# A local-attention and star-ReLU feed-forward kernel: hand-fixed issue order, DMA transposes, and the position bias added by TensorE

## The chip, the cores and the metric

The kernel runs on one core of a Trainium2 chip. The metric is device time in microseconds (us) for one execution. The span that a profile prints (first to last instruction) is about 2 us shorter than that time. An execution is called *slow* when it is over 1.5% above the fastest of the same kernel, otherwise *fast*. The engines are named as in the profile: PE is TensorE, PEld its weight loads (which overlap PE: 155.4 and 242.9 us busy in a span of 263.5 before), DVE is VectorE, ACT is ScalarE, POOL is GpSimd, SP is SyncE. An engine with a q (SPq, POOLq) is the engine issuing DMAs.

## The reference, cut to what matters

Four batches, 8 heads, 768 positions, 64 elements a head. A query sees the first 8 positions (global) and the 96 positions up to itself (local), with a linear penalty on distance that depends on the head. The attention output, put together over the heads to 3072 rows of 512, goes through a two-layer feed-forward network.

```python
scores = q @ k.T / 8
keep   = (pos_k < 8) | ((rel >= 0) & (rel < 96))        # rel = pos_q - pos_k
dist   = where(global and not local, 96, |rel|)
scores = where(keep, scores - slope[h] * dist, -1e9)     # slope[h] = 2 ** -(h + 1)
a      = softmax(scores)
x      = (a @ v) put together over heads                 # 3072 x 512
h      = x @ w_in                                        # 512 -> 2048
out    = (s * relu(h) ** 2 + b) @ w_out                  # 2048 -> 512
```

## The kernel before

It works on 12 *granules*: 256 query positions of one batch, all 8 heads, so 3 granules a batch. A granule is done in four *steps*, one for each pair of heads. In a step PE transposes q and k of the pair that comes two steps later, makes the scores of the next pair, multiplies probabilities and values for this one, and does a quarter of the hidden layer (P1) of the granule before and a quarter of the output layer (P2) of the one before that. The instructions are written in this order, and a scheduler may move them.

```python
    for s in range(NSTEP):                       # four steps a granule
        jm, qd = s // HP, s % HP
        if qd == 0:
            load_granule(*pend_loads.pop(0))     # GpSimd queue, fp32 to bf16
            make_voff(jm + 1)
        run_S(s + 1)                             # scores, exp, times template
        moe_p1(jm - 1, 2 * qd)
        mms, norm = stage_A(s); mms(); norm()    # probabilities x values
        moe_p1(jm - 1, 2 * qd + 1)
        run_T(s + 2)                             # 4 PE transposes, DVE evacuates
        moe_p2(jm - 2, qd // 2, qd % 2)
    # [conditions at the ends cut]

    # stage_A: lhsT, loaded into PE beforehand as its weights, is called stationary; rhs moves
    # here the values are stationary (64 columns: half the array), 128 queries move
    nc.tensor.matmul(av[hi*D:(hi+1)*D, i*P:(i+1)*P], lhsT=vv,
                     rhs=pts[hi][:, c*P:(c+1)*P], ...)          # 8 a step
    # ... and again with ones, for the row sums
    nc.tensor.matmul(av[hi*D:(hi+1)*D, GT+i*P:GT+(i+1)*P], lhsT=ones_bf[:, 0:D],
                     rhs=pts[hi][:, c*P:(c+1)*P], ...)          # 8 a step
    # norm: xT = av * exp(-ln(sum)), already transposed for P1
    nc.scalar.activation(lg[:], av[:, GT:2*GT], ACT.Ln)
    nc.scalar.activation(rc[:], lg[:], ACT.Exp, scale=-1.0)
    nc.vector.tensor_tensor(xT[j][:, hp, :], av[:, 0:GT], rc[:], ALU.mult)

    # start: the loads are one queue, in this order
    load_granule(0, 0)
    for i in range(4): load_w_in(i, 4)
    # [8 templates exp(-slope * dist) on ACT]
    load_granule(0, 1)
    for i in range(4): load_w_out(i, 4)
    load_granule(0, 2)
```

The softmax here doesn't subtract the row's maximum and nothing guards it: scores larger than these inputs give would overflow.

Of the kernel before, what the change touches and what calls it, by code (L numbers as in the profile page):

```python
# [8 lines left out]
F32 = mybir.dt.float32  # L9
# [4 lines left out]
NEG_BIG = -30000.0  # L14


@with_exitstack
def kernel(
# [23 lines left out]
    NGR = S // GT  # L42
    HP = H // 2
# [3 lines left out]
    NU = NJ * HP  # L47
# [8 lines left out]
    ldp = ctx.enter_context(tc.tile_pool(name="ldp", bufs=2))  # L56
    qkp = ctx.enter_context(tc.tile_pool(name="qkp", bufs=2))
    work = ctx.enter_context(tc.tile_pool(name="work", bufs=3))
    ppool = ctx.enter_context(tc.tile_pool(name="ppool", bufs=8))
    gpool = ctx.enter_context(tc.tile_pool(name="gpool", bufs=2))  # L60
    xpool = ctx.enter_context(tc.tile_pool(name="xpool", bufs=3))
    ps_sc = ctx.enter_context(tc.tile_pool(name="ps_sc", bufs=3, space=bass.MemoryType.PSUM))
    ps_av = ctx.enter_context(tc.tile_pool(name="ps_av", bufs=2, space=bass.MemoryType.PSUM))
    ps_h = ctx.enter_context(tc.tile_pool(name="ps_h", bufs=3, space=bass.MemoryType.PSUM))

    nc.scalar.preload_act_table_set("natural_log_exp_and_others")


    nat = {}
    for b in range(B):  # L70
        for nm in ("q", "k", "v"):
            nat[nm, b] = None

    def load(nm, src, b, g, h0, nh):
        key = (nm, b)
        if nat[key] is None:
            nat[key] = ldp.tile([P, S // P, H, D], BF16, name=f"{nm}nat", tag=f"{nm}nat")
        t = nat[key]
        for sb in range(g * GB, (g + 1) * GB):
            nc.gpsimd.dma_start(  # L80
                t[:, sb, h0 : h0 + nh, :],
                src[b, h0 : h0 + nh, sb * P : (sb + 1) * P, :].rearrange("h p d -> p h d"),
            )
# [4 lines left out]
    w_out_view = moe_w_out.rearrange("(fc p) c -> p fc c", p=P)  # L88

# [6 lines left out]
    def load_w_out(i, n):  # L96
        w = FC // n
        nc.gpsimd.dma_start(
            w_out_bf[:, i * w : (i + 1) * w, :], w_out_view[:, i * w : (i + 1) * w, :]
        )  # L100

    def load_granule(b, g, parts=1):
        n = H // parts
        for h0 in range(0, H, n):
            load("k", k, b, g, h0, n)
            load("q", q, b, g, h0, n)
            load("v", v, b, g, h0, n)

    s_bc = const.tile([P, 1], F32, name="s_bc")
    nc.sync.dma_start(s_bc[:], moe_s.to_broadcast((P, 1)))  # L110
    b_bc = const.tile([P, 1], F32, name="b_bc")
    nc.sync.dma_start(b_bc[:], moe_b.to_broadcast((P, 1)))

    ident_bf = const.tile([P, P], BF16, name="ident_bf")
    make_identity(nc, ident_bf[:])
    ones_bf = const.tile([P, P], BF16, name="ones_bf")
    nc.vector.memset(ones_bf[:], 1.0)


    base = const.tile([P, 5, P], F32, name="base")  # L120
# [8 lines left out]

# [8 lines left out]
    )  # L138
    nc.gpsimd.affine_select(
        out=rel[:],  # L140
# [7 lines left out]
    load_granule(0, 0)  # L148
    for i in range(4):
        load_w_in(i, 4)  # L150

    for i in (0, 1, 4):
        nc.vector.tensor_copy(base[:, i, :], rel[:, 0:P])
    for i in (2, 3):
        nc.vector.tensor_copy(base[:, i, :], rel[:, P : 2 * P])
    nc.vector.tensor_scalar_max(base[0:NG, 0, :], base[0:NG, 0, :], -float(NL))
    nc.vector.memset(base[0:NG, 2:4, :], -float(NL))

    tmpl = []
    for h in range(H):  # L160
        t = const.tile([P, 5 * P], BF16, name=f"tmpl{h}", tag=f"tmpl{h}")
        slope = float(2.0 ** (-8.0 * (h + 1) / H))
        nc.scalar.activation(
            t[:], base[:].rearrange("p a c -> p (a c)"), ACT.Exp, scale=slope
        )
        tmpl.append(t)

    load_granule(0, 1)
    for i in range(4):
        load_w_out(i, 4)  # L170
    load_granule(0, 2)


    st = {}
    qk = {}
    xT = {}
    gT = {}

    def unit(u):
        j, hp = divmod(u, HP)  # L180
        b, g = divmod(j, NGR)
        return j, hp, b, g

    voff_tiles = {}

    def make_voff(j):
        b, g = divmod(j, NGR)
        vn = nat["v", b]
        if g == 0:
            return  # L190
        vo = work.tile([P, GB, H, D], BF16, name="voff", tag="voff", bufs=2)
        nc.vector.tensor_copy(vo[:], vn[:, g * GB - 1 : (g + 1) * GB - 1, :, :])
        for i in range(GB):
            nc.vector.tensor_copy(vo[0:NG, i, :, :], vn[0:NG, 0, :, :])
        voff_tiles[j] = vo

    def stage_T(u):
        j, hp, b, g = unit(u)
        ps = ps_h.tile([P, 4 * P], BF16, name="ps_t", tag="psh")
        qn, kn = nat["q", b], nat["k", b]  # L200
        ops = []
        for i in range(GB):
            ops.append(
                lambda i=i: nc.tensor.transpose(  # L204
                    ps[:, (GB + i) * P : (GB + i + 1) * P],
                    kn[:, g * GB + i, 2 * hp : 2 * hp + 2, :],
                    ident_bf[:],
                )
            )
        for i in range(GB):  # L210
            ops.append(
                lambda i=i: nc.tensor.transpose(  # L212
                    ps[:, i * P : (i + 1) * P],
                    qn[:, g * GB + i, 2 * hp : 2 * hp + 2, :],
                    ident_bf[:],
                )
            )
        t = qkp.tile([P, 4 * P], BF16, name="qk", tag=f"qk{hp}_{g}")
        qk[b, g, hp] = t

        def evac():
            nc.vector.tensor_copy(t[:], ps[:])  # L222
            if g > 0:
                ko = work.tile([P, GB, P], BF16, name="koff", tag="koff", bufs=4)
                prev = qk[b, g - 1, hp]
                nc.vector.tensor_copy(ko[:, 0, NG:], prev[:, 3 * P + NG : 4 * P])  # L226
                nc.vector.tensor_copy(ko[:, 1, NG:], t[:, 2 * P + NG : 3 * P])
                first = qk[b, 0, hp]
                nc.vector.tensor_copy(
                    ko[:, :, 0:NG],  # L230
                    first[:, 2 * P : 2 * P + NG].unsqueeze(1).to_broadcast((P, GB, NG)),
                )
                st[u] = {"ko": ko}
            else:
                st[u] = {}

        return ops, evac



    def stage_S(u):
        j, hp, b, g = unit(u)
        t = qk[b, g, hp]
        first = g == 0
        ncol = 3 * P if first else 4 * P
        pss = [ps_sc.tile([P, 4 * P], F32, name="ps_s", tag="sc") for _ in range(2)]
        pts = [ppool.tile([P, 4 * P], BF16, name="pt", tag="pt") for _ in range(2)]
        st[u]["pt"] = pts

        def mms():  # L250
            if first:
                plan = [
                    (t, 2 * P, 0, 0),
                    (t, 3 * P, P, 1),
                    (t, 2 * P, P, 2),
                ]
            else:
                ko = st[u]["ko"][:].rearrange("p a c -> p (a c)")
                plan = [
                    (t, 2 * P, 0, 0),  # L260
                    (t, 3 * P, P, 3),
                    (ko, 0, 0, 1),
                    (ko, P, P, 2),
                ]
            for kt, kc0, qc0, oc in plan:
                for hi in range(2):
                    r0 = hi * D
                    nc.tensor.matmul(  # L268
                        pss[hi][:, oc * P : (oc + 1) * P],
                        lhsT=kt[r0 : r0 + D, kc0 : kc0 + P],  # L270
                        rhs=t[r0 : r0 + D, qc0 : qc0 + P],
                        start=True,
                        stop=True,
                    )

        def post(hi):
            h = 2 * hp + hi
            nc.scalar.activation(  # L278
                pts[hi][:, 0:ncol], pss[hi][:, 0:ncol], ACT.Exp, scale=QSCALE
            )  # L280
            m = tmpl[h][:, 0 : 3 * P] if first else tmpl[h][:, P : 5 * P]
            nc.vector.tensor_tensor(  # L282
                pts[hi][:, 0:ncol], pts[hi][:, 0:ncol], m, ALU.mult
            )

        return mms, [lambda: post(0), lambda: post(1)]

    def stage_A(u):
        j, hp, b, g = unit(u)
        first = g == 0  # L290
        pts = st[u]["pt"]
        vn = nat["v", b]
        vo = None if first else voff_tiles[j]
        av = ps_av.tile([P, 4 * P], F32, name="ps_av", tag="av")
        if j not in xT:
            xT[j] = xpool.tile([P, KC, GT], BF16, name="xT", tag="xT")
# [118 lines left out]
    def run_T(u):  # L415
        ops, evac = stage_T(u)
        for op in ops:
            op()
# [71 lines left out]
```

## Time and profile before

| | us |
|---|---|
| time, first listing (median of 3; lowest to highest) | 263.11 (263.06 to 266.51) |
| span of the profiled run | 263.5 |
| first P1 matmul starts | 23.55 |
| length of a step, 80 to 230 us | 4.80 (19.2 a granule) |
| last P2 matmul ends | about 259 |

These are lines of the page of the kernel before: busy time by engine, the busy tenths of PE and of DMA in 40 slices of 6.6 us, the granted clock, and the chain of work that ended last.

```profile
PE 242.9 (92%) x2376; PEld 155.4 (59%) x2416; DVE 152.7 (58%) x441; ACT 144.7 (55%) x297; POOL 71.1 (27%) x89
...
PE   0573999999999999999999999999999999999993
...
PEclk9999999999999999999999999999999999999998
DMA  6999999999991100159990110110011011011112
...
PE 89%; DMA 5%; POOL 3%; issue 1%; DVE 0%; ACT 0%; POOLq 0%
```

PE is busy 92% of the span and makes up 89% of the chain. No other engine is above 59%. So PE's own work is the time, apart from the start: PE is at 0, 5, 7 and 3 tenths in the first four slices. The chain in order of time names the reason (start, length, what):

```profile
10.59 12.72 DMA knat<-in_k_dram
```

The k of granule 1 stands in the queue behind all of w_in, and the chain holds 12.7 us from the issue of its load to its landing at 23.3. In this time PE still has some work; it stands idle for the last 4.6 us (its starts are at 18.49 and 23.36). The 9s of the PEclk row are misleading early on. The records of the granted clock begin at 39.6 us; before that P1 and transposes start twice as far apart as later (128-column matmuls 107 ns instead of 55 to 56), so PE ran at half its later rate.

The window 150 to 200 us gives busy time for PE, PEld, DVE, ACT, POOL (instruction counts in brackets), then granted clock, DMA share and GB/s:

```profile
150.00:200.00 50.00, 49.52 (x520) 32.32 (x529) 32.51 (x95) 30.94 (x65) 0.00 (x0) 1.00 0.08 28
```

PE is busy 49.5 of 50 us. This is one step there, PE only (start, length, line, operation, output<-inputs, shape, count):

```profile
153.62 0.28 PE L268 MATMUL ps_s<-qk 64*128 64x128 bf16 x4
...
153.94 1.05 PE L355 MATMUL ps_2471<-xT,w_in_bf 128*128 128x256 bf16 x8
154.92 0.25 PE L316 MATMUL ps_av<-pt,vnat 128*64 128x128 bf16 x2
...
155.17 0.39 PE L329 MATMUL ps_av<-pt,ones_bf 128*64 128x128 bf16 x8
155.49 1.05 PE L355 MATMUL ps_2504<-xT,w_in_bf 128*128 128x256 bf16 x8
156.38 0.28 PE L204 MATMUL ps_t<-ident_bf,knat 128*128 128x128 bf16 x2
156.49 0.28 PE L212 MATMUL ps_t<-ident_bf,qnat 128*128 128x128 bf16 x2
156.60 1.89 PE L389 MATMUL ps_2526<-w_out_bf,gT 128*128 128x512 bf16 x7
158.42 0.28 PE L268 MATMUL ps_s<-qk 64*128 64x128 bf16 x4
```

Read the starts, not the lengths (the ends are modelled and overlap). The 16 matmuls for values and row sums (L316, L329) take from 154.92 to 155.49, 0.57 us. The transposes (L204, L212) take 0.22 us. Where half-array matmuls (64 in one dimension of the tile) meet full ones, the next start comes 0.15 to 0.20 us later instead of 0.06 to 0.11: at 153.94 after the scores, for example.

### The profile page before, as it was taken

How to read it: one execution, taken by the hardware profiler on the slowest of the kernel's cores; microseconds unless marked ns; L12 is line 12 of the kernel's file. 1: busy time of each engine (PE TensorE's matmuls, PEld its weight loads, DVE VectorE, ACT ScalarE, POOL GpSimd, SP SyncE). 2: the span in 40 equal slices, each digit the busy share in tenths (PEclk: the TensorE clock that was granted, in tenths of full speed). 3: DMA queues.
4: the chain of work that ended last, by engine and by line, in shares of the span. 5: the costliest groups of instructions: out<-in, count | busy, mean ns of one | idle time of the engine just before them, and what ended most of it. 6: DMA issues, size and time to landing. Idle time of an engine off the chain costs nothing.

```text
span 263.5 us, 5861 instructions
## 1 busy us (share of the span) xinstructions
PE 242.9 (92%) x2376; PEld 155.4 (59%) x2416; DVE 152.7 (58%) x441; ACT 144.7 (55%) x297; POOL 71.1 (27%) x89
## 2 busy tenths in 40 slices
PE   0573999999999999999999999999999999999993
PEld 0352565756666566666666666656666566666641
DVE  2440746777856676577575676567657567543331
ACT  4770454857557476575665756646556466463310
POOL 9945649859910000069700000000000000000000
PEclk9999999999999999999999999999999999999998
DMA  6999999999991100159990110110011011011112
GB/s 43 145 206 167 206 182 155 151 110 141 160 141 40 44 29 14 40 36 164 179 106 0 44 40 2 40 42 21 21 40 44 0 42 44 0 42 40 40 42 80
DMA packets 82875, 20.31 MB, mean 77 GB/s; under 512 B 75680, under 2 KB 79776, under 8 KB 82848
## 3 DMA queue, kind: packets, MB, share of 16 engines
q0 software_dynamic: 79104, 13.64, 69.3%
q1 hardware_dynamic: 3744, 6.29, 6.5%
q8 instruction: 19, 0.31, 0.5%
q14 instruction: 8, 0.07, 0.1%
HBM read 27.26 MB, written 6.29 MB: 127 GB/s over the span
## 4 chain that ended last, share of the span: by engine, by line
PE 89%; DMA 5%; POOL 3%; issue 1%; DVE 0%; ACT 0%; POOLq 0%
PE ps_s L268 6%; PE ps_av L316 6%; DMA knat<-in_k_dram 5%; PE ps_av L329 4%; PE ps_t L204 2%; PE ps_t L212 2%; PE ps_3986 L389 1%; PE ps_4006 L389 1%; PE ps_3944 L389 1%; PE ps_3006 L389 1%; PE ps_1081 L389 1%; PE ps_b L371 1%; PE ps_2048 L389 1%; PE ps_3880 L389 1%; PE ps_3793 L389 1%; PE ps_3642 L389 1%
## 5 line engine op out<-in xcount | busy, mean ns | idle before, releaser
L278 ACT ACTIVATE pt<-ps_s 128x512 bf16<-128x512 f32 (+1 forms) x96 | 49.0, 559 | 70.2 <-PE ps_s L268 70.1
L355 PEld LDWEIGHTS <-w_in_bf 128*128 128x128 bf16 x768 | 69.4, 100 | 18.4 <-issue 1.4
L389 PEld LDWEIGHTS <-gT 128*128 128x128 bf16 x384 | 36.0, 98 | 35.0
L364 DVE TENSOR_TENSOR gT<-gT 128x512 bf16<-128x512 bf16 x96 | 40.7, 424 | 22.8 <-ACT gT L363 21.0
L80 POOL DMA_DIRECT2D knat<-in_k_dram x24 | 21.9, 930 | 47.4 <-PE ps_t L212 44.1
L342 DVE TENSOR_TENSOR xT<-ps_av,rc 128x256 bf16<-128x256 f32 x48 | 20.3, 422 | 13.7 <-ACT rc L341 13.7
L204 PE MATMUL ps_t<-ident_bf,knat 128*128 128x128 bf16 x96 | 14.5, 233 | 11.1 <-DMA knat<-in_k_dram 11.1
L222 DVE COPY qk<-ps_t 128x512 bf16<-128x512 bf16 x48 | 19.7, 415 | 7.9 <-PE ps_t L212 7.9
L80 POOL DMA_DIRECT2D vnat<-in_v_dram x24 | 21.2, 908 | 6.3 <-DMA w_in_bf<-in_moe_w_in_dram 2.6
L80 POOL DMA_DIRECT2D qnat<-in_q_dram x24 | 21.5, 913 | 0.4 <-issue 0.3
L341 ACT ACTIVATE rc<-lg 128x256 f32<-128x256 f32 x48 | 20.0, 416 | 1.4
L316 PE MATMUL ps_av<-pt,vnat 128*64 128x128 bf16 x224 | 19.6, 241 | 1.2 <-DVE pt L282 0.7
L268 PEld LDWEIGHTS <-qk 64*128 64x128 bf16 x224 | 7.6, 97 | 21.1 <-issue 16.2
L339 ACT ACTIVATE lg<-ps_av 128x256 f32<-128x256 f32 x48 | 18.4, 383 | 2.5 <-PE ps_av L329 2.5
L329 PE MATMUL ps_av<-pt,ones_bf 128*64 128x128 bf16 x352 | 19.5, 230 | 0.0
L268 PE MATMUL ps_s<-qk 64*128 64x128 bf16 x224 | 17.8, 233 | 0.3 <-DVE qk L222 0.3
L204 PEld LDWEIGHTS <-knat 128*128 128x128 bf16 x96 | 9.5, 102 | 13.5 <-DMA knat<-in_k_dram 11.6
L316 PEld LDWEIGHTS <-vnat 128*64 128x64 bf16 x224 | 10.7, 114 | 11.1 <-issue 10.6
L212 PE MATMUL ps_t<-ident_bf,qnat 128*128 128x128 bf16 x96 | 14.3, 234 | 1.3 <-DMA qnat<-in_q_dram 1.3
L329 PEld LDWEIGHTS <-ones_bf 128*64 128x64 bf16 x352 | 14.1, 118 | 0.0
L226 DVE COPY koff<-qk 128x120 bf16<-128x120 bf16 x32 | 7.3, 234 | 8.9 <-PE ps_s L268 8.9
L282 DVE TENSOR_TENSOR pt<-pt,tmpl_136 128x512 bf16<-128x512 bf16 (+1 forms) x12 | 4.8, 403 | 11.5 <-ACT pt L278 11.5
(284 smaller groups left out, 389.7 us busy)
## 6 DMA issues: line engine op xcount, KB each, us to landing
out_dram<-o_sb SPq DMA_DIRECT2D x24, 256.0 KB, 2.0
knat<-in_k_dram POOLq DMA_DIRECT2D x24, 128.0 KB, 6.5
qnat<-in_q_dram POOLq DMA_DIRECT2D x24, 128.0 KB, 6.5
vnat<-in_v_dram POOLq DMA_DIRECT2D x24, 128.0 KB, 6.7
w_in_bf<-in_moe_w_in_dram POOLq DMA_DIRECT2D x4, 512.0 KB, 9.9
w_out_bf<-in_moe_w_out_dram POOLq DMA_DIRECT2D x4, 512.0 KB, 10.7
s_bc<-in_moe_s_dram SPq DMA_DIRECT2D x1, 0.5 KB, 2.8
b_bc<-in_moe_b_dram SPq DMA_DIRECT2D x1, 0.5 KB, 2.9
```

Source lines behind the costliest of these rows:

```text
L80: nc.gpsimd.dma_start(t[:, sb, h0 : h0 + nh, :], src[b, h0 : h0 + nh, sb * P : (sb + 1) * P, :].rearrange("h p d -> p h d"),)
L204: lambda i=i: nc.tensor.transpose(ps[:, (GB + i) * P : (GB + i + 1) * P], kn[:, g * GB + i, 2 * hp : 2 * hp + 2, :], ident_bf[:],)
L222: nc.vector.tensor_copy(t[:], ps[:])
L268: nc.tensor.matmul(pss[hi][:, oc * P : (oc + 1) * P], lhsT=kt[r0 : r0 + D, kc0 : kc0 + P], rhs=t[r0 : r0 + D, qc0 : qc0 + P], start=True, ...
L278: nc.scalar.activation(pts[hi][:, 0:ncol], pss[hi][:, 0:ncol], ACT.Exp, scale=QSCALE)
L316: nc.tensor.matmul(av[hi * D : (hi + 1) * D, i * P : (i + 1) * P], lhsT=vv, rhs=pts[hi][:, c * P : (c + 1) * P], start=not off, stop=bool( ...
L329: nc.tensor.matmul(av[hi * D : (hi + 1) * D, GT + i * P : GT + (i + 1) * P], lhsT=ones_bf[:, 0:D], rhs=pts[hi][:, c * P : (c + 1) * P], st ...
L341: nc.scalar.activation(rc[:], lg[:], ACT.Exp, scale=-1.0)
L342: nc.vector.tensor_tensor(xT[j][:, hp, :], av[:, 0:GT], rc[:], ALU.mult)
L355: nc.tensor.matmul(ps[:, i, :], lhsT=w_in_bf[:, kc, fc * P : (fc + 1) * P], rhs=xT[j][:, kc, :], start=(kc == 0), stop=(kc == KC - 1),)
L364: nc.vector.tensor_tensor(gs, gs, gs, ALU.mult)
L389: nc.tensor.matmul(po[:], lhsT=gT[j][:, fc, tb * P : (tb + 1) * P], rhs=w_out_bf[:, fc, :], start=(fc == 0), stop=(fc == FC - 1),)
```

## The change

The intent is to shorten the period and the start at once:

1. **Issue order by hand.** The order of the whole program is written out, and the scheduler is switched off. One *period* a granule replaces four steps.
2. **q and k transposes move to DMA**, two granules ahead, on SP's queue, from granule 3 on.
3. **Probabilities become stationary.** The output is queries by 65: 64 values and a 65th column of ones, which yields the row sum. Full-array matmuls, half as many, and a 4-column reciprocal on DVE in place of Ln and Exp on ACT. The result now has queries on partitions, so it must be transposed for P1: two more DMA transposes a granule (`xT`).
4. **Start.** Granule 1 loads before w_in, w_in comes in eighths; q and k of granules 0 to 2 are loaded in 512-byte runs (two positions at once); for granules 0 and 1 PE adds the position bias into PSUM with a scaled identity, so no template is multiplied; dummy matmuls before the first work are meant to end the half rate early.
5. **Output bias.** The sum over w_out is added up on DVE and finished with 2 matmuls instead of 16; POOL adds it to the first four output tiles, whose P2 finishes before it is known.

```diff
+    ctx.enter_context(tc.manual_schedule())
@@ loads at the start
-    load_granule(0, 0)
-    for i in range(4):
-        load_w_in(i, 4)
+    load_pairs(0, "k")  ...  load_pairs(0, "q")  ...  load_v(0)
+    load_pairs(1, "k"); load_pairs(1, "q"); load_v(1)
+    for i in range(8):
+        load_w_in(i, 8)
+    load_pairs(2, "k"); load_pairs(2, "q"); load_v(2)
+    # [w_out in quarters, granule 3]
+    load_granule(4)
@@ position bias of granules 0 and 1
+            nc.tensor.matmul(ps[:, hi, 0:n], lhsT=diag[:, 2 * hp + hi, :], rhs=m, start=True, stop=False)
@@ transposes of q and k (k shown)
-        nc.tensor.transpose(ps[...], kn[:, g * GB + i, 2 * hp : 2 * hp + 2, :], ident_bf[:])
+            nc.sync.dma_start_transpose(
+                kT[b][:, :, sb * P : (sb + 1) * P],
+                nat["k", j][:, i, :, :].rearrange("p h d -> p (h d)"))
@@ attention
-        nc.tensor.matmul(av[...], lhsT=vv,               rhs=pts[hi][:, c * P : (c + 1) * P], ...)
-        nc.tensor.matmul(av[...], lhsT=ones_bf[:, 0:D],  rhs=pts[hi][:, c * P : (c + 1) * P], ...)
+        nc.tensor.matmul(av[:, i, hi, :], lhsT=pt[:, hi, c * P : (c + 1) * P], rhs=vv, ...)   # 65 columns
-        nc.scalar.activation(lg[:], av[:, GT : 2 * GT], ACT.Ln)
-        nc.scalar.activation(rc[:], lg[:], ACT.Exp, scale=-1.0)
+        nc.vector.reciprocal(rc[:], av[:, :, :, D : D + 1])
+    def XT_dma(j):                                       # attention output, one granule
+        for i in range(GB):
+            nc.sync.dma_start_transpose(xT[j][:, :, i * P : (i + 1) * P], xn[j][:, i, :, :]...)
@@ the period
+    def period(j, items, at, late=None):
+        if j + 3 < NJ:
+            load_granule(j + 3)
+        SS(j, (0, 1)); run(items, at[0]); A(j, 0); run(items, at[1]); A(j, 1)
+        KO(j + 1); VO(j + 1)
+        SS(j, (2, 3)); run(items, at[2]); A(j, 2); run(items, at[3]); A(j, 3)
+        XT_dma(j)
+        XB(j + 2)                                        # q, k transposes by DMA
+        if late is not None: late()                      # output bias, granules 0, 1
+        run(items, 100)                                  # items: P1 of j-1, P2 of j-2 and j-1
```

(`...` and brackets mark cuts, and conditions at the ends are left out.)

## The prediction

It was written with the trace before and the diff at hand, before anything of the change was built.

> **What bounds it now.** TensorE. The page: PE busy 92% of 263.5 us, the chain 89% PE; DVE 58%, ACT 55%. From 80 to 230 us the windows have PE busy 98-99%; the timeline there repeats a step of 4.80 us, four steps a granule: 19.2 us, 12 granules. From matmul starts: 64 hidden-layer matmuls (256 columns) at 109 ns = 7.0 us; 32 output matmuls (512 columns) about 216 ns = 6.9; scores 16 pairs at 56 ns = 0.9; attention-value and ones-sums 32 pairs at 56 = 1.8; 16 transposes at 56 = 0.9. Sum 17.5. The other 1.7 us: entering or leaving half-array matmuls (scores, and values and sums) shows starts 0.15-0.20 us apart instead of 0.06-0.11. [...]four changes a step.
> The rest is the start: the chain has 12.7 us waiting for k of granule 1, behind all of w_in; the first hidden-layer matmul is at 23.5 us; starts are twice as far apart (107 ns instead of 56) until 39.6 us.
>
> **What changes.**
> - Steady PE: transposes go to DMA (-0.9 us a granule). Probabilities stationary: 32 full-array matmuls of 65 columns replace 64 half-array ones, the ones-sums going into a 65th column. The trace has a weight load plus 128-column matmul each 55 ns; for 65 columns I estimate 35-55 ns, so 1.1-1.8 us, against 1.8. Tiling changes fall from 16 to 4 (-1.2 us). Ideal 16.3-17.0 us a granule; with some stalls 17.1 (-2.1).
> - Ln and Exp normalisation (ACT 383+416 ns) becomes a small DVE reciprocal. DVE per granule, from durations: about 12 us; ACT about 9; neither binds a 17 us period.
> - Output bias sum: 16 matmuls of 512 (3.5 us) become 2.
> - Start: granule 1 loads before w_in; w_in in eighths lets the first hidden-layer pair begin after one eighth. Before, q/k/v of a granule moved in about 5 us, w_in in 10. So the first eighth lands about 12-13 us, the last about 21. 512-byte runs halve q/k packets early: 1-2 us. [...]PE bias removes early template multiplies, but ACT is busy: dense PE work from about 15-16 us.
> - New DMA: six transposes of 128 KB per granule on SP. No transpose is in this trace; stores of 256 KB land in 2.0 us. [...]k/q are two granules ahead. Only attention output (two in sequence) is tight: between the last attention matmuls and its first use lie about 6 us of PE work. I allow 0.5 us of stall per granule.
>
> **Sum.** 15.5 + hidden and output work 167 + attention of 10 granules 27 + granules 1-2 extras, transposes, bias 6 + start stalls 4 + transpose stalls 4 + tail 4.3 (as before) = 228 us. Range 219 to 241. Faster by over 2% 0.91; within 2% 0.05; slower 0.04.
>
> **What would show it.** First hidden-layer matmul near 15 us; twice-as-far starts ending well before 39 us; period of 16.5-17.5 us; no PE transposes after granule 2; fewer 0.15-0.20 us gaps; 65-column matmuls 35-55 ns apart; PE waits on attention-output transposes under 1 us each.
>
> **What would make it wrong.** Transposes landing in over 5 us, or SP issuing them slowly, stalls every granule; single-buffered score or output PSUM stalling a fixed order; weights arriving late, leaving PE holes up to 40 us.

The sum: 15.5 + 167 + 27 + 6 + 4 + 4 + 4.3 = 227.8, given as 228 us. Two of its figures are estimates: the 0.5 us of stall a granule, made with one landing time at hand (2.0 us for a store), and the 1 to 2 us for 512-byte runs (half the packets of q and k, in loads that took about 5 us a granule).

## The result, and the profile after

| | before | changed |
|---|---|---|
| time, us (median; lowest to highest) | 264.31 (263.06 to 266.51) | 236.58 (232.74 to 239.12) |
| ratio of fast runs | 1 | 0.886 (0.875 to 0.896) |
| first P1 matmul starts | 23.55 | 17.67 |
| period of a granule, steady part | 19.2 | 16.1 to 16.6 |
| PE waiting for `xT` | none | 8.8 |

A ratio is the mean time of one kernel's fast runs over the mean of the other's fast runs of the same rounds, with a 95% interval, so it isn't quite the ratio of the medians in the table. The changed kernel is 10 to 12.5% faster. Its own runs scatter more than those of any other kernel here: 237.22, 235.95, 239.12 and 232.74, with a mean granted clock of 0.971, 0.975, 0.961 and 0.992. The scatter is in the clock: span times (1 - clock), an estimate of the time lost to half rate, is 6.8, 5.9, 9.3 and 1.8 us, and without it the four spans are within 228.0 to 229.2 us. Two of the runs, the profiled one included, count as slow, so its share of half rate is higher than that of a fast run. What I read from this profile I therefore also looked for in fast profiles: one with different load runs at the start (`rows`, below) shows the same three waits.

The page of the changed kernel, the lines that answer to those of before (slices of 5.9 us):

```profile
PE 212.3 (90%) x1967; PEld 141.6 (60%) x1997; DVE 135.0 (57%) x311; ACT 115.1 (49%) x173; POOL 76.4 (32%) x95
...
PE   5899999985988899399999999999999999999993
...
PEclk9799999996799999979999999999999999999999
DMA  6999999999992899999589599423504413013102
...
PE 72%; DMA 10%; DVE 10%; ACT 3%; issue 3%; SPq 0%; DVEq 0%; POOLq 0%
```

PE's work fell from 242.9 to 212.3 us. PE is busy from the first slice, but there are now gaps in slices 10, 13 and 17. The clock is lower in slices 10, 11 and 18, right after, and in slice 2 (half rate from 6.9 to 10.3 us). Two entries of the chain have grown: DMA from 5 to 10%, DVE from 0 to 10%. In the steady part the window and the timeline of PE read:

```profile
150.00:200.00 50.00, 48.49 (x464) 33.93 (x471) 31.12 (x75) 25.73 (x37) 0.00 (x0) 1.00 0.33 82
```

```profile
160.25 0.19 PE L385 MATMUL ps_av<-vaug,pt 128*128 128x65 bf16 x1
160.28 0.20 PE L385 MATMUL ps_av<-vo,pt 128*128 128x65 bf16 x1
...
160.47 0.19 PE L385 MATMUL ps_av<-vo,pt 128*128 128x65 bf16 x1
160.50 1.91 PE L432 MATMUL ps<-xT,w_in_bf 128*128 128x256 bf16 x16
162.46 2.54 PE L473 MATMUL ps<-w_out_bf,gT 128*128 128x512 bf16 x11
```

The eight matmuls of a pair of heads take from 160.25 to 160.50, 0.25 us instead of 0.57, each with a fresh stationary tile and 29 to 35 ns apart. The long P2 group at 162.46 recurs at 178.58, 195.16 and 211.69 in the chain: a period of 16.1, 16.6 and 16.5 us.

What is left is in the list of waits of PE (total, times, longest):

```profile
PE ps L432 <- DMA xT<-xn: 8.8, 3, 4.0
PE ps L473 <- DVE o_sb L484: 3.2, 10, 0.5
```

All of the 8.8 us fall before 98 us: PE starts are 3.87 us apart at 51.8, 1.66 at 75.5 and 4.35 at 93.7. This is the last of the three, all engines (timeline, most lines cut):

```profile
88.46 1.81 POOL L103 DMA_DIRECT2D knat<-in_k_dram  x2
88.73 2.57 SPq L419 DMA_TRANSPOSE xT<-xn  x2
...
89.70 2.54 PE L473 MATMUL ps<-w_out_bf,gT 128*128 128x512 bf16 x11
90.19 1.83 POOL L103 DMA_DIRECT2D qnat<-in_q_dram  x2
...
91.92 1.85 POOL L111 DMA_DIRECT2D vaug<-in_v_dram  x2
...
93.08 1.02 PE L473 MATMUL ps<-w_out_bf,gT 128*128 128x512 bf16 x4 [0.29 <-DVE o_sb L484]
...
98.08 0.60 PE L432 MATMUL ps<-xT,w_in_bf 128*128 128x256 bf16 x4 [3.97 <-DMA xT<-xn]
```

SP issues the two `xT` transposes of granule 4 from 88.73 on, and at the same moment POOL issues the six loads of granule 7 (k, q, v). PE runs out of other work at about 94.1 and stands until 98.08. The DMA view says what these transposes need as a rule (issues, median us to landing):

```profile
xT<-xn SPq DMA_TRANSPOSE x20, 2.5
kT<-knat SPq DMA_TRANSPOSE x18, 3.1
qT<-qnat SPq DMA_TRANSPOSE x18, 3.5
```

The median of 2.5 us would have brought the second of them, issued at 89.98, home at 92.5, before PE needed it. It landed at 97.9. Each pair, with the packets of loads (GpSimd queue) that moved while it was under way, counted in the DMA records of the trace:

| `xT` of granule | issued at, us | landed after, us | load packets meanwhile |
|---|---|---|---|
| 2 | 46.01, 47.24 | 7.79, 8.41 | 5,622, 5,977 |
| 3 | 73.32, 74.56 | 2.42, 2.48 | 0, 16 |
| 4 | 88.73, 89.98 | 6.85, 7.96 | 4,972, 6,102 |
| 5 to 11 | | 2.4 to 3.1 | at most 268 |

The three waits are not all alike. The pair of granule 3 landed fast, beside no loads, and PE still waited 1.3 us for it:

```profile
73.32 2.51 SPq L419 DMA_TRANSPOSE xT<-xn  x2
...
77.18 1.03 PE L432 MATMUL ps<-xT,w_in_bf 128*128 128x256 bf16 x8 [1.29 <-DMA xT<-xn]
```

From the issue of its second transpose (74.56) to the end of PE's other work lie 1.3 us; in granule 4 it was 4.1 us. So this wait is one of a short lead, and 7.5 of the 8.8 us belong to the two slow pairs. In those SP's issue took 1.2 to 1.3 us each, as in the others: the transfer was slow, not the issue.

So the landing time about triples (6.85 to 8.41 us against 2.42 to 2.48) beside 5,000 to 6,000 packets of another queue. By what rule packets of the two queues take turns isn't in the trace, and what it shows is not an even alternation: with the pair of granule 2 under way, no packet of SP's queue started from 47.94 to 50.49 us, while some 2,900 load packets did. The granted clock shows a second cost. It falls to 0.5 at 54.7 for 6.8 us, near the end of the first long hole, and at 99.0 for 3.4 us, just after the second. In both stretches P1 matmuls start 213 ns apart instead of 109. At half rate 10.2 us cost about 5 us (estimate: half of 10.2).

The theory after the result: **the loads of later granules, issued when a pair of `xT` transposes is under way, delay them, PE waits, and its clock can halve afterwards; with the wait of granule 3 together about 14 us in this run (8.8 plus 5).** A first rival says that the waits are only a matter of too short a lead, whatever else moves. A second says that the period and the start, not the holes, decide the time, so that removing the holes changes little.

### The profile page after: what moved, and what is told of

It is laid out like the page before. It is cut to its first block, busy times and chain, and to the rows that moved or that the text cites. A ratio compares the mean times of both kernels' runs of the same rounds, so it can differ in the third digit from the quotient of the medians.

```text
span 235.4 us, 4869 instructions
## 1 busy us (share of the span) xinstructions
PE 212.3 (90%) x1967; PEld 141.6 (60%) x1997; DVE 135.0 (57%) x311; ACT 115.1 (49%) x173; POOL 76.4 (32%) x95
## 4 chain that ended last, share of the span: by engine, by line
PE 72%; DMA 10%; DVE 10%; ACT 3%; issue 3%; SPq 0%; DVEq 0%; POOLq 0%
PE ps L432 33%; PE ps L473 25%; DMA xT<-xn 8%; PE ps_av L385 5%; PE ps_s L340 3%; PE ps_2s L473 3%; DVE o_sb L484 3%; ACT gT L440 2%; DMA knat<-in_k_dram 2%; PE ps_s L324 2%; PE ps_t L235 1%; DVE gT L441 1%; DVE pt L357 1%; DVE ko L284 1%; DVE vo L298 1%
## 5 line engine op out<-in xcount | busy, mean ns | idle before, releaser
L432 PE MATMUL ps<-xT,w_in_bf 128*128 128x256 bf16 x768 | 98.2, 279 | 8.8 <-DMA xT<-xn 8.8
L440 ACT ACTIVATE gT<-ps 128x512 bf16<-128x512 f32 x96 | 57.3, 598 | 76.4 <-PE ps L432 75.6
L473 PE MATMUL ps<-w_out_bf,gT 128*128 128x512 bf16 x309 | 78.7, 381 | 5.1 <-DVE o_sb L484 3.2
L353 ACT ACTIVATE pt<-ps_s 128x1024 bf16<-128x1024 f32 (+1 forms) x48 | 43.4, 951 | 22.9 <-PE ps_s L340 22.6
L357 DVE TENSOR_TENSOR pt<-pt,tmpl 128x1024 bf16<-128x1024 bf16 (+1 forms) x40 | 26.6, 675 | 9.5 <-ACT pt L353 8.8
L111 POOL DMA_DIRECT2D vaug<-in_v_dram x24 | 21.3, 902 | 7.6 <-DMA qnat<-in_q_dram 3.3
L484 DVE SCALAR_TENSOR_TENSOR o_sb<-ps,s_bc,bvec 128x512 f32<-128x512 f32 x18 | 13.4, 744 | 14.0 <-PE ps L473 13.9
L394 DVE TENSOR_TENSOR xn<-ps_av,rc 128x256 bf16<-128x256 f32 x48 | 20.4, 424 | 1.7
L385 PEld LDWEIGHTS <-pt 128*128 128x128 bf16 x352 | 15.9, 98 | 7.2 <-DVE xn L394 4.2
L385 PE MATMUL ps_av<-vaug,pt 128*128 128x65 bf16 x224 | 17.8, 195 | 0.8 <-DVE xn L394 0.6
L103 POOL DMA_DIRECT2D qnat<-in_q_dram x18 | 16.1, 905 | 4.9 <-DMA qT<-qnat 1.9
## 6 DMA issues: line engine op xcount, KB each, us to landing
w_out_bf<-in_moe_w_out_dram POOLq DMA_DIRECT2D x4, 512.0 KB, 12.7
```

The costliest lines, as they stand in the source:

```text
L103: nc.gpsimd.dma_start(t[:, i, :, :], src[b, :, sb * P : (sb + 1) * P, :].rearrange("h p d -> p h d"))
L111: nc.gpsimd.dma_start(vaug[b][:, sb, :, 0:D], v[b, :, sb * P : (sb + 1) * P, :].rearrange("h p d -> p h d"),)
L353: nc.scalar.activation(pt[:, :, 0:n], ps[:, :, 0:n], ACT.Exp, scale=QSCALE)
L357: nc.vector.tensor_tensor(pt[:, :, 0:n], pt[:, :, 0:n], m, ALU.mult)
L385: nc.tensor.matmul(av[:, i, hi, :], lhsT=pt[:, hi, c * P : (c + 1) * P], rhs=vv, start=n_ == 0, stop=n_ == len(ops) - 1,)
L394: nc.vector.tensor_tensor(xn[j][:, :, 2 * hp : 2 * hp + 2, :], av[:, :, :, 0:D], rc[:].to_broadcast((P, GB, 2, D)), ALU.mult,)
```

## The experiments

All twelve are edits of the changed kernel, and all give correct results. Each was timed in rounds with the kernel before on the same chip, and ratios are to that kernel. The median of the kernel before was 263.67 to 264.31. Intervals are 95%; for the changed kernel itself the ratio is 0.886 (0.875 to 0.896). The median of the changed kernel holds its two slow runs, so the last column gives the difference to it by fast runs alone: the difference of the two ratios times 264 us, good to about 3 us either way. Where the text names both, this is the one to go by.

| run | what | median us | ratio (interval) | to changed, fast runs, us |
|---|---|---|---|---|
| hold4 | loads of granule 4 after `xT` of 2 | 235.31 | 0.892 (0.888 to 0.896) | +1.7 |
| load7 | loads of granule 7 one period earlier | 235.05 | 0.891 (0.886 to 0.897) | +1.4 |
| both | both | 237.07 | 0.895 (0.887 to 0.903) | +2.4 |
| xtpe | `xT` of 2, 3, 4 transposed by PE | 230.21 | 0.871 (0.865 to 0.876) | -4.0 |
| holdall | every load after the `xT` of its period | 229.17 | 0.867 (0.863 to 0.871) | -5.0 |
| noorder | scheduler chooses the order | 269.73 | 1.017 (1.010 to 1.025) | +34.7 |
| rows | no 512-byte runs | 237.97 | 0.901 (0.895 to 0.907) | +4.0 |
| kqpe | q, k transposed by PE throughout | 247.04 | 0.934 (0.929 to 0.939) | +12.7 |
| nobias | no bias on PE, templates throughout | 241.86 | 0.915 (0.911 to 0.919) | +7.7 |
| noidle | no dummy matmuls | 237.35 | 0.896 (0.891 to 0.901) | +2.8 |
| dvebias | POOL's four bias additions on DVE | 234.75 | 0.889 (0.885 to 0.893) | +0.8 |
| best | holdall and dvebias | 226.17 | 0.859 (0.853 to 0.865) | -7.2 |

### hold4, load7 and both: move the colliding loads

hold4 takes granule 4's loads from the start and puts them behind the `xT` of granule 2, which POOL waits for by copying one row of it. load7 issues the loads of granule 7 a period earlier, so that they are over before the `xT` of granule 4. Both does both.

```diff
# hold4
     load_v(3)
-    load_granule(4)
     ...
     XT_dma(2)
+    nc.gpsimd.tensor_copy(held[:], xT[2][0:1, 0, :])
+    load_granule(4)
# load7
-        if j + 3 < NJ:
+        if j + 3 < NJ and j != 4:
             load_granule(j + 3)
     ...
         if late is not None:
+            load_granule(j + 4)
             late()
```

> Granule 4's loads are issued only after the attention-output transposes of granule 2 have landed. Theory A (contention: those transposes took 8.4 us because granule loads filled the same 16 DMA engines; alone they take 2.5): they land in under 4 us, the 3.5 us PE wait near 52 us falls under 1 us and the half-rate clock stretch after it (6.8 us at half rate, 3.4 us lost) goes: 4 to 8 us faster than the changed kernel's 236, so 228 to 232; the 4.0 us wait near 94 us stays. Rival B (the first transposes on the queue are slow by themselves, or the queue's order delays them): landing stays near 8 us, time within 1 us.

> Granule 7's loads stand ahead of the bias work on the GpSimd queue, so they are done before the transposes of granule 4. Theory A: those land in about 2.5 us instead of 8, the 4.0 us PE wait near 94 us and the half-rate stretch after it (1.7 us lost) go: 4 to 6 us faster, 230 to 232; the wait near 52 us stays. Rival B: no change beyond 1 us.

> Both moves. Theory A: both waits go, 8 to 13 us faster than the changed kernel, 223 to 228[...]. Rival B: within 2 us of 236.

The time didn't move: all three are within the interval of the changed kernel. In hold4 the targeted wait at 52 us was gone and in load7 the one at 94; in both the first was gone and the second only fell from 4.0 to 1.8 us. In each another came. The wait line of each (the profile of both is of a slow run), first hold4, then load7, then both:

```profile
PE ps L431 <- DMA xT<-xn: 5.7, 2, 4.6
```

```profile
PE ps L432 <- DMA xT<-xn: 8.6, 2, 5.5
```

```profile
PE ps L431 <- DMA xT<-xn: 6.9, 2, 5.1
```

The landing times say why (us, both transposes of each pair):

| `xT` of granule | changed | hold4 | load7 | both |
|---|---|---|---|---|
| 2 | 7.79, 8.41 | 3.65, 2.50 | 7.67, 8.07 | 3.95, 2.50 |
| 3 | 2.42, 2.48 | 6.39, 6.89 | 6.83, 6.69 | 6.54, 7.35 |
| 4 | 6.85, 7.96 | 5.90, 5.09 | 2.42, 2.48 | 6.86, 5.82 |

In hold4 5,592 and 6,104 load packets moved beside the pair of granule 3, and 3,246 and 2,475 beside that of granule 4, whose landing times lie in between. So the loads that were moved away from one pair ran into the next, and the hole that followed was longer (5.0 us in hold4, 5.9 in load7, 5.4 in both, each around 71 to 73 us) with 10.2 us at half clock again. My expectation of a gain failed in all three. The mechanism isn't hurt by it: the delay went with the loads, to the pair that they met. The "short lead" rival is hurt for the long waits: in load7 granule 4's pair came in the same place of the same fixed order, landed in 2.4 us beside no load packet, and PE didn't wait for it.

### xtpe: no DMA transpose of `xT` where the loads are dense

```diff
-    XT_dma(2)
     P2_mm(0, 0, 3)
+    XT_pe(2, "act", "av")
     ...
         A(j, 3)
-        XT_dma(j)
+        if j > 4:
+            XT_dma(j)
     ...                                  # one item later:
+        if j <= 4:
+            XT_pe(j, "act", "av")
```

> Granules 2 to 4 transpose their attention output on TensorE and evacuate on ScalarE; the DMA order is as in the changed kernel. Both theories: the waits on these transposes vanish; 0.45 us of PE is paid back per granule: 7 to 12 us faster, 224 to 229. If weights or other data are late too (rival C: the PE would wait for another load right behind), less than 3 us is gained.

It ran in 230.2, a little above what I expected: 4.0 us below the changed kernel by fast runs, with intervals that just touch (6.4 us by medians). No wait for an `xT` transpose is left, and the half-rate time fell from 10.2 to 3.4 us. What is left is a different hole of 3 us at 76.4. The timeline there, DVE, POOL and the PE line that ends it:

```profile
76.45 2.29 DVE L441 TENSOR_TENSOR gT<-gT 128x512 bf16<-128x512 bf16 x2
...
76.84 1.27 POOL L505 TENSOR_TENSOR o_sb<-o_sb,bvec 128x512 f32<-128x512 f32 x1
...
79.35 0.20 PE L385 MATMUL ps_av<-vaug,pt 128*128 128x65 bf16 x1 [2.70 <-DVE xn L394]
```

Two DVE squarings of 0.43 us each took 2.29 us together, while POOL added the output bias. In the same way a DVE multiplication beside POOL's addition took 1.83 instead of 0.69 us in the changed kernel. In dvebias (below), where POOL adds nothing, two such multiplications took 1.28 us together. So these DVE operations were slower beside POOL's additions; by what mechanism wasn't shown.

### holdall: every load waits for the transposes of its period

```diff
-        if j + 3 < NJ:
-            load_granule(j + 3)          # at the start of the period
     ...
         XT_dma(j)
+        if j + 3 < NJ:
+            hold(j)                      # POOL copies one row of xT[j]
+            load_granule(j + 3)
```

(After the `xT` of granule 2 the loads of granules 4 and 5 follow in the same way.)

> The loads of each granule from 4 on are issued only after the attention-output transposes of an earlier granule have landed, so that no such transpose has bulk loads outstanding beside it. Theory A (contention on the 16 DMA engines; the single moves only passed the collision on to the next granule): every attention-output transpose lands in under 4 us, PE waits on them under 1.7 us each, time 225 to 231. Rival C (the loads themselves are the limit: whatever is held back is missed later): transposes land fast but new PE holes appear behind later loads or k/q transposes, time stays 233 to 238.

It ran in 229.2, with all runs between 228.9 and 229.3, so the scatter is gone too. The lines of the tile `xT` and of the wait:

```profile
DMA to landing us min/median/max: 2.4/2.5/4.1
```

```profile
PE ps_av L388 <- DVE pt L360: 2.0, 1, 2.0
...
PE ps L435 <- DMA xT<-xn: 1.4, 1, 1.4
```

The slowest of 20 transposes landed in 4.1 us instead of 8.4, and PE's wait fell from 8.8 to 1.4 us. The gain of 5.0 us by fast runs (7.4 by medians), with intervals clear of each other, is the direct test of the theory: the transposes are the same, the same loads move, only not at once. It falls against the second rival. The 1.4 us that are left are granule 3's wait again (at 70.8 us, its pair landing in 3.1 and 2.5 us), which is the part that the short lead explains. Of the about 14 us of holes and half rate, not all came back: there is a 2.0 us wait behind DVE (beside POOL's bias additions again: a DVE copy of 8x1040 took 2.09 us there, 0.43 and 0.68 without an addition in the changed kernel), 3.4 us of half rate follow it at 83.1, and in this profile the start has 6.8 us of half rate (8.0 to 14.8) where the changed kernel's had 3.4.

### noorder: the scheduler decides

```diff
-    ctx.enter_context(tc.manual_schedule())
+    pass
```

> The same instructions, but the scheduler chooses the order instead of the hand-written one. If the fixed order is worth something by itself: slower than 236 by 3 to 20 us, with PE waits on exp, multiply and normalisation inside each period. If the gain is only in the removed work: within 3 us of 236.

With the same operations in the scheduler's order the kernel takes 269.7 us, more than the kernel before. In the window 150 to 200 PE's busy time is about that of the changed kernel (48.8 against 48.5 us) and the period is 16.5 us: the loss is before about 130 us, in two holes of 14.5 and 14.1 us for `xT` above all, and in the half rate that goes with them (mean granted clock 0.903, an estimated 26 us against 6.8). SP's timeline shows how:

```profile
75.57 3.13 SPq L419 DMA_TRANSPOSE xT<-xn  x2
78.79 25.82 SPq L265 DMA_TRANSPOSE kT<-knat  x8
...
110.15 2.52 SPq L419 DMA_TRANSPOSE xT<-xn  x2
```

In this timeline SP issues one transpose after the other. The transposes of k (25.8 us for 8) wait for their loads, and the next `xT` transposes, at 110.15, stand behind them, while PE has nothing else. In the hand-fixed order the `xT` transposes stand ahead of those of k and q. So the order is worth 33 to 35 us to these operations; the prediction had given it no term, since it took the written order as given.

### rows: no 512-byte runs

```diff
-    load_pairs(0, "k")                   # and q, and granules 1, 2
+    load_rows(0, "k")
```

(The transposes and evacuations of these granules take plain rows then, without reordering two positions.)

> q and k of granules 0 to 2 in 256-byte runs again (rows on partitions as before), so their evacuation needs no de-interleaving either. The prediction gave the 512-byte runs 1 to 2 us: first hidden-layer matmul 0.5 to 2 us later than 17.7, time 236 to 239; but evacuations of 512 columns become about 0.25 us shorter each, so the net may be zero.

The first P1 matmul started at 20.2 instead of 17.7 us, because the first eighth of w_in landed at 20.1 instead of 16.7 (16.3 to 17.1 in all runs with the 512-byte runs and the written order; the first P1 itself lies between 16.7 and 19.6 in those that keep this start and the dummy matmuls and bias). The time rose by 1.4 us in the medians and 4.0 by fast runs, and the intervals touch. So the runs bring the start forward; how much of it reaches the end isn't settled, because the evacuation changed with them. This is the fast profile with the three waits of the changed kernel (7.9 us in three).

### kqpe: q and k transposed by PE throughout

```diff
-            XB(j + 2)                    # DMA transposes
+            for half in range(2):
+                run(items, 1)
+                TT(j + 2, half)          # 16 PE transposes, DVE and ACT evacuate
```

(All q and k loads take 512-byte runs here, which is what the PE transposes expect.)

> q and k of all granules transposed on TensorE instead of by DMA (and all loaded in 512-byte runs). By PE time: 16 pairs of half-array matmuls at 56 ns and the tiling changes, 1.1 to 1.4 us more per period, 17.6 to 18 us instead of 16.5, so 8 to 11 us slower: 243 to 248. Against that, fewer load packets and no k/q transposes beside the attention-output ones: up to 6 us back, 238 to 242.

It is 12.7 us slower by fast runs (10.5 by medians), with a period of 18.5 to 18.8 instead of 16.5 us. PE lines of one half of a granule's transposes:

```profile
129.36 0.41 PE L235 MATMUL ps_t<-ident,knat 128*64 128x128 bf16 x8 [0.70 <-ACT qT L253]
129.58 0.42 PE L235 MATMUL ps_t<-ident,qnat 128*64 128x128 bf16 x8
130.16 2.10 PE L479 MATMUL ps<-w_out_bf,gT 128*128 128x512 bf16 x9 [0.16 <-issue]
```

The 16 transposes take 0.8 us, twice a granule, and PE waits 0.7 us for the evacuation before them. So DMA transposes of q and k are worth 2.0 to 2.3 us a granule against this form. Against the form of the kernel before (16 whole transposes, 0.9 us) the worth is less: these are half-array ones, twice as many.

### nobias and noidle: two parts of the start

```diff
# nobias: granules 0, 1 as all others
-    SB_mm(0, 0)
-    SB_mm(0, 1)
+    make_tmpl(1)
     ...
-        S_mm(0, hp, True)
-        S_post(0, hp, True)
+        S_mm(0, hp)
+        S_post(0, hp)
+        make_tmpl(2 * hp + 2)
+        make_tmpl(2 * hp + 3)
# noidle
-    idle(9)
     ...
-    idle(2)
```

> Granules 0 and 1 get their position bias by multiplied templates as the others do, instead of 16 matmuls; the templates of all heads are made at the start on ScalarE (0.74 us each, 5.9 us), the diagonals (8 of 0.29 us) are not made. If the PE bias is worth what the prediction supposed (ScalarE and VectorE bind the start): first hidden-layer matmul 2 to 4 us later than 17.7 us, time 238 to 241. If the start is bound by loads instead (w_in's first eighth lands at 16.8 us): within 1.5 us of 236.

> Without the 11 dummy matmuls. If they warm the clock: half rate lasts longer at the start, up to 15 to 20 us, and the kernel is 1 to 4 us slower, 237 to 240. If real matmuls warm it as early: within 1 us of 236.

Without the bias on PE the kernel is 7.7 us slower by fast runs (5.3 by medians). The templates (0.67 us each on ACT) stand between the first exponentials, the first P1 starts at 22.4 instead of 17.7, and PE runs at half rate from 7.2 to 24.2 us. So PE bias is worth about 5 to 8 us. Without the dummy matmuls the difference is 0.8 us by medians and 2.8 by fast runs, with overlapping intervals: no effect shown.

### dvebias and best

dvebias takes POOL's four bias additions to DVE and their stores from POOL's queue to SP's. best is holdall with this.

```diff
-        nc.gpsimd.tensor_tensor(o_sb[:], o_sb[:], bvec[:], ALU.add)
+        nc.vector.tensor_tensor(o_sb[:], o_sb[:], bvec[:], ALU.add)
     ...
-        nc.gpsimd.dma_start(out[t0 : t0 + P, :], o_sb[:])
+        nc.sync.dma_start(out[t0 : t0 + P, :], o_sb[:])
```

> The four late bias additions (and their stores) of granules 0 and 1 go from GpSimd to VectorE (stores on SP); nothing else changes. In the changed kernel a VectorE multiply beside a GpSimd addition took 1.83 us instead of 0.69. If GpSimd's reads hold VectorE up: no stretched VectorE instruction is left between 74 and 83 us; but granule 7's loads also move earlier, as in the load7 run, and may collide with granule 3's transposes. Time 232 to 237.

> Loads held behind the attention-output transposes (as in holdall) and the late bias additions on VectorE instead of GpSimd. If GpSimd's reads caused the 2.2 us PE hole at 80 us and the half-rate stretch after it: 2 to 4 us faster than holdall's 229.2, 225 to 228. If they are not the cause: 228 to 230.

dvebias alone brings nothing that can be told from scatter (0.889 against 0.886). There are two reasons in its profile. A POOL without additions issues the loads of granule 7 earlier, and they then meet the `xT` of granule 3 (landing in 6.8 and 6.1 us). And the four additions, 2.5 us on DVE from 71.25 on, hold up an output evacuation for which PE then waits 3.6 us; half rate from 74.2 to 81.1 follows. Together with holdall it brings 2 to 3 us more than holdall alone (226.2 against 229.2; the intervals overlap by a little, so this step is likely rather than shown). Lines of the page and the waits of best:

```profile
PE   6698998999894999999999999999999999999992
...
PEclk9999999999999999999999999999999999999999
```

```profile
PE ps_s L343 <- DMA qT<-qnat: 2.3, 1, 2.3
...
PE ps L435 <- DMA xT<-xn: 0.3, 1, 0.3
```

The clock is full from 4.2 to 222.7 us, and PE waits 0.3 us for `xT`. The largest single wait left is 2.3 us for a q transpose at 70 us, whose load is issued later now. best is faster than both kernels: 14.1% below the kernel before (ratio 0.859), and 7.2 us below the changed kernel by fast runs (10.4 by medians).

## Why the prediction was right or wrong

The prediction of 228.0 (219 to 241), faster with 0.91, held: 236.58, inside the range but 8.6 us above its sum. That the total came this close owes something to luck: one term was 10 us too small, and two were some 5 us too large together. Its terms, point by point:

- **PE bounds the kernel, and the period shrinks.** Right. It said 17.1 us a granule "with some stalls", 16.3 to 17.0 without. Measured: 16.1 to 16.6, so the steady part has no stalls. The 17.1 include stalls; the sum itself counts stalls apart and takes 16.6 (167 over 12 granules, plus 2.7 of attention). Against that, 8 to 9 steady periods of about 16.4 are some 2 us in favour of the kernel.
- **65-column matmuls 35 to 55 ns apart.** A little too cautious: 29 to 35 ns, although each has a fresh stationary tile. A head pair takes 0.25 instead of 0.57 us, 1.3 us a granule.
- **Tiling changes cost.** Seen in the trace before, where starts are 0.15 to 0.20 us apart at a change instead of 0.06 to 0.11; why wasn't shown. That fewer changes are worth 1.2 us was not tested alone; only the sum of the three PE savings (19.2 to 16.1 to 16.6) is measured.
- **Start: "dense PE work from about 15-16 us".** Mis-sized: 17.7 us. The sum took the first eighth of w_in at 12 to 13 us; it landed at 16.75. This costs 2.2 us against the 15.5 of the sum. The 4 us of start stalls were over-sized: from 17.67 to 50 us PE is idle for 0.9 us. The part that PE bias plays was right in kind; nobias gives it 5 to 8 us.
- **"transpose stalls 4" (0.5 us a granule).** This is the term that failed. It measured three waits with 8.8 us and none later, plus about 5 us of half rate that the prediction had no term for: about 14 in the profiled run. The lead was foreseen well (about 6 us of PE work; in granule 4 6.4 us, from 87.71 to 94.11), the landing time was not. The mechanism was on its list of what would make it wrong ("Transposes landing in over 5 us ... stalls every granule"), but with a wrong scope: here they took over 5 us (6.85 to 8.41) only with loads under way, so of ten granules two stall for long, one for 1.3 us and seven not at all. The allowance was the author's estimate, beside 2.0 us for a store of 256 KB before. On a quiet queue the transposes came near that (2.4 to 2.5 us for 128 KB); the allowance didn't ask what else moves. holdall showed it: the same transposes, 4.1 us at most, 5.0 us less time by fast runs (7.4 by medians).
- **"Only attention output ... is tight".** Right: the waits for k and q transposes are absent from PE's list, that for `xT` leads it.

The sum with measured terms: 228 + 2.2 (start) - 3 (start stalls, 0.9 instead of 4) - 2 (period) + 10 (transposes, 14 instead of 4) = 235, against a span of 235.4 and a time of 237.2 in the profiled run.

Left open: what w_in in eighths, the stationary probabilities and the new bias sum bring each by itself (no run changed one alone), and what the 512-byte runs bring to the end of the kernel. That the loads are what triples the landing time is argued from packet counts, from the moving delay, from stretches in which only load packets start and from holdall; by what mechanism they delay the transposes is not seen.

## What to carry to other kernels

When work moves from an engine to DMA, ask for each such transfer how much other work lies before its first use, and which loads are issued in that time: here the transfer with a short lead landed in 2.4 to 2.5 us with no or few loads under way and in 6.85 to 8.41 us beside them, and the loads with a long lead could wait for it (one small copy on the loading engine, worth 5 to 7 us). Moving one load aside only handed the collision to the next transfer here (hold4: 6.39 and 6.89 us for granule 3's pair instead of 2.42 and 2.48); make the rule hold for all of them. And reckon that a stall of PE may cost twice, once for the wait and once for the half clock after it: a hole of 2.2 us in holdall was followed by 3.4 us at half rate. Whether half rate follows went here with how busy PE was in a window of 3.41 us (last section).

## What the traces showed of transposes, the clock and weight loads

- A transpose of 128 KB between SBUF tiles took 2.4 to 2.5 us to land on a quiet queue, which is about 53 GB/s for it alone (an estimate: 128 KB in 2.45 us); the first 1.2 us of this are SP's issue. Beside 4,000 to 6,600 packets of loads on another queue it took 6.4 to 8.4 us in the changed kernel, hold4, load7 and both.
- The length of a gap of PE alone did not decide whether half rate followed: holes of 2.2 us (holdall, at 80.2) and 3.0 us (xtpe, at 76.4) were followed by 3.4 us at half rate, holes of 3.5 us (load7, at 51.8) and 3.3 us (rows, at 54.3) were not. What orders all 14 traces is PE's busy share in fixed windows. Each full-rate stretch of the clock's records lasts a whole multiple of 3.41 us (3.41, 44.37, 37.55 and 133.12 us in the changed kernel). Cut into windows of that length, the 33 full-rate windows that half rate followed have PE busy for at most 46% of their time, and the other 852 for at least 44.6%. In the changed kernel, up to PE's last matmul, these are 38, 28 and 28% (windows from 3.46, 51.25 and 95.62 us) and at least 47%.
- Weight load and matmul pairs at 128 columns (the transposes of the kernel before, 4 in a row) start 55 to 57 ns apart at full rate, and at 65 columns with a fresh 128-column weight load (8 in a row, changed kernel) 29 to 35 ns.
- The clock row of the profile shows full rate before the first record of the granted clock: in the kernel before that was at 39.6 us, with starts 107 ns apart until then.
